# A decode block with a gated MLP on one core: not computing the first layer norm, the product with w1 and its gelu

## The chip, the cores and the metric

The kernel runs on one core of a Trainium2 chip. The metric is the device time of one execution in microseconds (us), lower is better.

## The reference, cut to what matters

```python
x = A_x                                    # (2, 1, 1024): two batch rows, ONE position each
g = sigmoid((x * gate_w).sum(-1, keepdims=True))
a = attention(x, A_k_cache, A_v_cache, A_wq, A_wo)     # 32 heads, 16384 cached keys of 128
b = mixer_mlp(x, B_w1, B_w2, B_w3, B_w4)
return g * a + (1 - g) * b

def mixer_mlp(x, w1, w2, w3, w4):
    B, S, D = x.shape                      # S == 1
    h = gelu(layernorm(x) @ w1)
    c = D // 4
    g0 = pad(h[:, :, 0*c:1*c], ((0,0),(1,0),(0,0)))[:, :S, :]   # shift by +1
    g1 = pad(h[:, :, 1*c:2*c], ((0,0),(0,1),(0,0)))[:, 1:, :]   # shift by -1
    g2 = pad(h[:, :, 2*c:3*c], ((0,0),(2,0),(0,0)))[:, :S, :]   # shift by +2
    g3 = pad(h[:, :, 3*c:   ], ((0,0),(0,2),(0,0)))[:, 2:, :]   # shift by -2
    hs = concatenate([g0, g1, g2, g3], -1) @ w2
    x1 = x + hs
    h2 = gelu(layernorm(x1) @ w3) @ w4
    return x1 + h2
```

All four shifts move along the position axis. With one position every row of `h` is shifted out and zeros come in. So `g0` to `g3` are zero for any `x` and `w1`. The K and V caches are the bulk of the data: 2 x 32 heads x 16384 x 128 in bf16 are 268 MB each. One head of one batch row is 4.19 MB of K and as much of V.

## The kernel before

The kernel walks 64 steps, one per head and batch row. A ring of five SBUF slots of 32 KB per partition (4 MB) takes every large load in a fixed order: K of step g, V of step g-1, and now and then a weight. One queue (SP) issues the loads. It waits for a slot to be released by the engine that read it last.

```python
wloads = {}
...
wloads[("w12", 0)] = [rows4(B_w1, 0, NHI, D), rows4(B_w2, 0, NHI, D, off=W12)]   # two loads, one slot
...
def release(key, ev):          # the slot goes to the next load in the list, which waits for ev
    idx = slot_of[key]
    slot_free[idx] = tuple(ev) if isinstance(ev, (tuple, list)) else (ev,)
    pump()
```

The small MLP is cut into stages that are put between the attention instructions of some steps, at five places of each step:

```python
MPOS = (1, 4, 7, 10, 13)
...
mg = 1
put(mg, [st_gate, ln_a(xT_f[:, :, :], "xT_f", st1_ps, "xn1"), ln_b(st1_ps, "xn1", None)])
mg += 1
key = ("w12", 0)
put(mg, mlp_chain(key, halves, 0, NBD, NBD, h_ps, lambda kc: xn_bf[:, kc, :], "xn1", "h", D, last=False)
    + [gelu1]
    + mlp_chain(key, halves, 0, NBD, NBD, hs_ps, lambda kc: shT_bf[:, kc, :], "const", "hs", D, off=W12), key)
mg += 1
put(mg, [st_x1, ln_a(x1T_f[:, :, :], "x1", st2_ps, "xn2"), ln_b(st2_ps, "xn2", "h")])
```

The kernel already uses constant zeros for the shifted rows (`shT_bf`, set once by a memset). It computes `h` all the same, and nobody reads its result. The slot of w1 and w2 is released by the last product with w2 (`last` is true by default), and K's slot by the last score matmul of the step:

```python
def do_S(g, u):
    ...
    if u == NU - 1:
        ev_S[g] = ev
        release(("k", g), ev)
```

Of the kernel before, what the change touches and what calls it, by code (L numbers as in the profile page):

```python
# [9 lines left out]
BF16 = mybir.dt.bfloat16  # L10
# [75 lines left out]
def build_kernel(nc, A_x, A_k, A_v, A_wq, A_wo, B_w1, B_w2, B_w3, B_w4, gate_w, out, dbg=None):  # L86
    dbg = dbg or {}
    B, Sq, D = A_x.shape
# [4 lines left out]
    P = 128  # L93
# [7 lines left out]
    NBD = D // P  # L101
    NBF = F // P
# [9 lines left out]
    NHI = NBD // R4  # L112
# [5 lines left out]
    with ExitStack() as st:  # L118
        block = st.enter_context(nc.Block())
        sb = lambda name, shape, dt: st.enter_context(nc.sbuf_tensor(name, shape, dt))  # L120
# [14 lines left out]
        xT_f = sb("xT_f", [P, NBD, 2], F32)  # L135
# [17 lines left out]
        mv = sb("mv", [P, 8], F32)  # L153
        zc = sb("zc", [P, NBD, 2], F32)
        xn_bf = sb("xn_bf", [P, NBD, 2], BF16)
        hT_bf = sb("hT_bf", [P, NBD, 2], BF16)
        shT_bf = sb("shT_bf", [P, NBD, 2], BF16)
        x1T_f = sb("x1T_f", [P, NBD, 2], F32)
        GT_bf = sb("GT_bf", [P, NBF, 2], BF16)
# [88 lines left out]
        def rows4(Wt, c0, cn, width, off=0):  # L248
            def fn(e, idx):
                src = Wt[c0 * R4 * P:(c0 + cn) * R4 * P, :].rearrange("(c p r) n -> p c (r n)", p=P, r=R4)  # L250
                dst = ring[:, idx, off:off + cn * R4 * width].rearrange("p (c m) -> p c m", c=cn)
                return e.dma_start(dst, src)
            return fn
# [9 lines left out]
                return e.dma_start(ring[:, idx, 0:hn * D].rearrange("p (h n) -> p h n", h=hn), src)  # L263
            return fn

        W12 = NBD * D
        wloads = {}
        for hi in range(NHI):
            wloads[("wq", hi)] = [rows4(A_wq, hi, 1, HD)]
            wloads[("w3", hi)] = [rows4(B_w3, hi, 1, F)]  # L270
        wloads[("w12", 0)] = [rows4(B_w1, 0, NHI, D), rows4(B_w2, 0, NHI, D, off=W12)]
        w4_parts = _split(NCF, 4)
        for pi, (k0, kn) in enumerate(w4_parts):
            wloads[("w4", pi)] = [rows4(B_w4, k0, kn, D)]
# [16 lines left out]
        B5 = banks[5]  # L291
        a_ps = B5[:, 0:2 * NBD].rearrange("p (n b) -> p n b", b=2)
        c0 = 2 * NBD
        g_ps = B5[:, c0:c0 + 2]; c0 += 4
        st1_ps = B5[:, c0:c0 + 4]; c0 += 4
        st2_ps = B5[:, c0:c0 + 4]; c0 += 4
        h_ps2d = B5[:, c0:c0 + 2 * NBD]; c0 += 2 * NBD
        hs_ps2d = B5[:, c0:c0 + 2 * NBD]; c0 += 2 * NBD
        h2_ps2d = B5[:, c0:c0 + 2 * NBD]; c0 += 2 * NBD
        h3_ps2d = B5[:, c0:c0 + 2 * NBF]; c0 += 2 * NBF  # L300
        assert c0 <= 512
        r3 = lambda ap2: ap2.rearrange("p (n b) -> p n b", b=2)
        h_ps, hs_ps, h2_ps, h3_ps = r3(h_ps2d), r3(hs_ps2d), r3(h2_ps2d), r3(h3_ps2d)
        bc_nb = lambda ap2: ap2.unsqueeze(1).broadcast_to([P, NBD, 2])
        b5_rd = []
        evd = {}
# [16 lines left out]
        def rd5(ev):  # L323
            b5_rd.append(ev)
            return ev
# [18 lines left out]
        def ln_a(z_ap, zkey, st_ps, tag):  # L344
            def run():
                zv = z_ap.rearrange("p n b -> p b n")
                a1 = pl.add("dve", lambda e: e.tensor_reduce(st_in[:, 0:2], zv, axis=AX.X, op=ALU.add),
                            waits=(evd[zkey], evd.get("ln_prev")), sig=True)
                a2 = mm5(st_ps[:, 0:2], ones_f[:, :], st_in[:, 0:2], waits=(a1, ev_const), sig=True)
                a3 = rd5(pl.add("dve", lambda e: e.tensor_scalar(mv[:, 0:2], st_ps[:, 0:2], 1.0 / D, None, op0=ALU.mult),  # L350
                                waits=(a2,) + rd5w(), sig=True))
                a4 = pl.add("dve", lambda e: e.tensor_tensor(zc[:, :, :], z_ap, bc_nb(mv[:, 0:2]), op=ALU.subtract),
                            waits=(a3, evd[zkey], evd.get("zc_free")), sig=True)
                a5 = pl.add("dve", lambda e: e.tensor_tensor(zz[:, 1, :, :], zc[:, :, :], zc[:, :, :], op=ALU.mult),
                            waits=(a4,), sig=True)
                evd[tag + "_a6"] = pl.add("dve", lambda e: e.tensor_reduce(st_in[:, 2:4], zz[:, 1, :, :].rearrange("p n b -> p b n"),
                                                                           axis=AX.X, op=ALU.add), waits=(a5,), sig=True)
                evd[tag + "_a4"] = a4
            return run

        def ln_b(st_ps, tag, xn_free_key):
            def run():
                a7 = mm5(st_ps[:, 2:4], ones_f[:, :], st_in[:, 2:4], waits=(evd[tag + "_a6"],), sig=True)
                a8 = rd5(pl.add("dve", lambda e: e.tensor_scalar(mv[:, 2:4], st_ps[:, 2:4], 1.0 / D, eps, op0=ALU.mult, op1=ALU.add),
                                waits=(a7,) + rd5w(), sig=True))
                a9 = pl.add("pool", lambda e: e.tensor_tensor(mv[:, 4:6], mv[:, 2:4], neg_half[:, :], op=ALU.pow),
                            waits=(a8, ev_const), sig=True)
                evd[tag] = pl.add("dve", lambda e: e.tensor_tensor(xn_bf[:, :, :], zc[:, :, :], bc_nb(mv[:, 4:6]), op=ALU.mult),
                                  waits=(a9, evd[tag + "_a4"], evd.get(xn_free_key)), sig=True)
                evd["ln_prev"] = evd[tag]  # L370
                evd["zc_free"] = evd[tag]
            return run

        def gelu_stage(src_ps2d, n, out_bf2d, src_key, out_key, extra_keys=()):
            def run():
                X = gl_x[:, 0:n]; A0 = gl_a[:, 0:n]; B0 = gl_b[:, 0:n]
                c = math.sqrt(2.0 / math.pi)
                b0 = rd5(pl.add("dve", lambda e: e.tensor_copy(out_bf2d, src_ps2d),
                                waits=(evd[src_key],) + tuple(evd.get(k) for k in extra_keys) + rd5w(), sig=True))
                b1 = pl.add("dve", lambda e: e.tensor_copy(X, out_bf2d), waits=(b0,), sig=True)  # L380
                b2 = pl.add("dve", lambda e: e.tensor_tensor(A0, X, X, op=ALU.mult), waits=(b1,), sig=True)
                b3 = pl.add("dve", lambda e: e.tensor_scalar(A0, A0, 0.044715, 1.0, op0=ALU.mult, op1=ALU.add), waits=(b2,), sig=True)
                b4 = pl.add("dve", lambda e: e.tensor_tensor(B0, A0, X, op=ALU.mult), waits=(b3,), sig=True)
                b5 = pl.add("act", lambda e: e.activation(A0, B0, ACT.Tanh, scale=c), waits=(b4,), sig=True)
                b6 = pl.add("dve", lambda e: e.tensor_scalar(B0, A0, 0.5, 0.5, op0=ALU.mult, op1=ALU.add), waits=(b5,), sig=True)
                evd[out_key] = pl.add("dve", lambda e: e.tensor_tensor(out_bf2d, B0, X, op=ALU.mult), waits=(b6,), sig=True)
            return run
# [38 lines left out]
                               waits=(c2, evd["g"]), sig=True)  # L426

        evd["const"] = ev_const
        gelu1 = gelu_stage(h_ps2d, 2 * NBD, hT_bf[:, :, :].rearrange("p n b -> p (n b)"), "h", "hT")
        gelu2 = gelu_stage(h3_ps2d, 2 * NBF, GT_bf[:, :, :].rearrange("p n b -> p (n b)"), "h3", "GT", ("hT",))  # L430
        MPOS = (1, 4, 7, 10, 13)
        stage_at = {}
        w_at = {}
# [1 line left out]
        def put(g, fns, key=None):  # L435
            if key is not None:
                w_at.setdefault(g, []).append(key)
            assert len(fns) <= len(MPOS)
            for pos, fn in zip(MPOS, fns):
                stage_at.setdefault((g, pos), []).append(fn)  # L440

        def mlp_chain(key, groups, k0, nkw, nout, out_ps, rhs_of, rhs_key, done_key, width, off=0, last=True):
            return [dense_stage(key, kls, k0, nkw, nout, out_ps, rhs_of, rhs_key, done_key, width, off,
                                last and i == len(groups) - 1) for i, kls in enumerate(groups)]

        halves = [list(range(0, NBD // 2)), list(range(NBD // 2, NBD))]
        mg = 1
        put(mg, [st_gate, ln_a(xT_f[:, :, :], "xT_f", st1_ps, "xn1"), ln_b(st1_ps, "xn1", None)])
        mg += 1
        key = ("w12", 0)  # L450
        put(mg, mlp_chain(key, halves, 0, NBD, NBD, h_ps, lambda kc: xn_bf[:, kc, :], "xn1", "h", D, last=False)
            + [gelu1]
            + mlp_chain(key, halves, 0, NBD, NBD, hs_ps, lambda kc: shT_bf[:, kc, :], "const", "hs", D, off=W12), key)
        mg += 1
        put(mg, [st_x1, ln_a(x1T_f[:, :, :], "x1", st2_ps, "xn2"), ln_b(st2_ps, "xn2", "h")])
        MSTEP = 2 if G >= 24 else 1
        for hi in range(NHI):
            mg += MSTEP
            key = ("w3", hi)
# [4 lines left out]
        for pi, (k0, kn) in enumerate(w4_parts):  # L464
            mg += MSTEP
            key = ("w4", pi)
# [40 lines left out]
        last = None  # L507
        for nb in range(NBD):
            last = pl.add("pe", lambda e, nb=nb: e.transpose(tr_ps[:, nb * 4:nb * 4 + 2], xrow4(xg_row, 2, nb), ident[0:2, 0:2]),
                          waits=(ev_x, ev_ident), sig=(nb == NBD - 1))  # L510
# [9 lines left out]
        for hi in range(NHI):  # L520
            key = ("wq", hi)
            ev_arr = arrived(key)
            wv = ring_w(slot_of[key], R4, HD)
            for r in range(R4):
                kc = hi * R4 + r
# [275 lines left out]
```

## Time and profile before

| | before |
|---|---|
| median of 4 runs | 1353.49 us (1352.82 to 1353.92) |
| profiled execution | 1352.0 us, span 1350.2 us |
| read from HBM | 572.53 MB, 424 GB/s over the span |
| PE, DVE, ACT busy | 64%, 56%, 7% |

How to read what follows. A trace tells when each instruction ran and what released it. PE is the matmul engine, DVE, ACT and POOL are the vector, scalar and general engines, SPq is the queue that issues loads. The span runs from the first to the last instruction. A large idle share of an engine says nothing by itself; what matters is which resource has no idle time.

These lines are from the page of the kernel before: the span, the busy share of the 16 DMA engines in 40 equal slices (9 is 90% or more), the total of the reads, the chain of waits that ended last, the transposes of K on DVE (busy us in all, mean ns of one, then DVE's idle time just before them and what ended it), and the two loads w1 and w2 (count, KB each, median us from issue to landing).

```profile
span 1350.2 us, 13016 instructions
...
DMA  9999999999999999999999999999999999999995
...
HBM read 572.53 MB, written 0.00 MB: 424 GB/s over the span
...
DMA 65%; PE 22%; DVE 12%; issue 1%; ACT 0%; SPq 0%; POOL 0%
...
L571 DVE STREAM_TRANSPOSE ring<-ring 128x1024 f32<-128x1024 f32 x512 | 591.7, 1212 | 153.3 <-DMA ring<-in_A_k_cache_dram 153.3
...
ring<-in_B_w_dram SPq DMA_DIRECT2D x2, 2048.0 KB, 43.9
```

DMA is at 9 tenths or more in 39 of 40 slices. The chain is 65% DMA although DMA has no idle slice before the last. The chain follows the data, and where it names PE or DVE, the DMA engines were moving later loads at the same time. The line of the transposes, the first thing done to each K, tells the same from the other side: DVE spent 153.3 us waiting for K to land.

This is the table of stretches of the kernel before. Each row is a stretch in us, its length, the busy time of PE, PE's weight loads, DVE, ACT and POOL with instruction counts, the granted PE clock (1.00 is full speed), the DMA share and GB/s.

```profile
40.00:60.00 20.00, 11.98 (x46) 5.32 (x43) 11.37 (x23) 0.95 (x3) 0.00 (x0) 0.81 0.99 420
60.00:80.00 20.00, 12.02 (x97) 5.40 (x98) 11.00 (x17) 1.38 (x3) 1.19 (x3) 0.76 1.04 443
80.00:100.00 20.00, 15.82 (x162) 7.63 (x163) 11.43 (x21) 1.59 (x4) 0.00 (x0) 0.75 0.99 425
100.00:120.00 20.00, 12.71 (x46) 5.26 (x48) 9.53 (x18) 0.00 (x0) 1.18 (x3) 0.57 1.00 430
400.00:600.00 200.00, 129.61 (x727) 48.17 (x728) 119.56 (x152) 13.76 (x30) 2.62 (x10) 0.83 1.00 431
```

The first four rows hold all the work that the change removes. The last row is the steady state. The DMA share does not tell them apart: it is 0.99 to 1.04 in the first four (a share over 1 cannot be real; presumably it comes from how records are cut at the edge of a stretch) and 1.00 in the last.

This is the timeline of the kernel before around the products with w1 (start, us, engine, line, operation; in brackets the idle time before it and what ended it), and at three later points.

```profile
67.79 0.33 SPq L286 DMA_DIRECT2D ring<-in_A_k_cache_dram  x1
...
73.25 2.37 DVE L571 STREAM_TRANSPOSE ring<-ring 128x1024 f32<-128x1024 f32 x2 [1.33 <-DMA ring<-in_A_k_cache_dram]
...
75.44 1.20 PE L403 MATMUL ps<-xn_bf,ring 128*128 128x2 bf16 x32
...
81.60 1.23 PE L403 MATMUL ps<-xn_bf,ring 128*128 128x2 bf16 x32
...
83.91 0.21 ACT L384 ACTIVATE gl_a<-gl_b 128x16 f32<-128x16 f32 x1 [11.86 <-DVE gl_b L383]
...
93.24 0.33 SPq L289 DMA_DIRECT2D ring<-in_A_v_cache_dram  x1
...
651.85 0.33 SPq L286 DMA_DIRECT2D ring<-in_A_k_cache_dram  x1
...
1341.31 1.91 PE L599 MATMUL ps<-ring,PT_sb 128*32 128x512 bf16 x32 [0.68 <-DMA ring<-in_A_v_cache_dram]
...
1348.58 0.27 SPq L731 DMA_DIRECT2D out_dram<-xg_row  x1
```

### The profile page before, as it was taken

The numbers are of one execution on the slowest core, as the hardware profiler recorded it, in microseconds if no ns is written. First come the engines' busy times: TensorE is split into PE (matmuls) and PEld (weight loads), VectorE is DVE, ScalarE is ACT, GpSimd is POOL, SyncE is SP. The second block draws the span as 40 slices with busy tenths as digits, with TensorE's granted clock in tenths as the row PEclk, the third lists the DMA queues.
The fourth block names the chain that finished last, engine by engine and source line by source line (L and its number), as shares of the span: only waits on it lengthen the run. The fifth ranks groups of instructions, "written<-read, shape, count | busy, mean of one in ns | idle before, by whom it ended". The sixth has DMA issues, their size and how long they took to land.

```text
span 1350.2 us, 13016 instructions
## 1 busy us (share of the span) xinstructions
PE 867.3 (64%) x5734; PEld 349.3 (26%) x5734; DVE 759.2 (56%) x1008; ACT 90.0 (7%) x196; POOL 23.9 (2%) x95
## 2 busy tenths in 40 slices
PE   2676767557666666766674666766666666567546
PEld 2232332223222222222222322222222222222223
DVE  0656455546656656665663656665565566566535
ACT  0000000000000000000000000000000000000000
POOL 1000000000000000000000000000000000000000
PEclk9777666786888878787976978787877887888868
DMA  9999999999999999999999999999999999999995
GB/s 403 427 431 430 432 431 424 435 426 432 432 433 425 432 433 432 429 430 432 432 415 432 429 433 432 430 429 433 432 431 429 432 434 431 429 431 432 415 424 254
DMA packets 24675, 573.38 MB, mean 425 GB/s; under 512 B 2213, under 2 KB 2213, under 8 KB 6314
## 3 DMA queue, kind: packets, MB, share of 16 engines
q1 hardware_dynamic: 24616, 572.54, 99.0%
q8 instruction: 45, 0.74, 0.2%
q14 instruction: 12, 0.10, 0.0%
q10 hardware_dynamic: 2, 0.00, 0.0%
HBM read 572.53 MB, written 0.00 MB: 424 GB/s over the span
## 4 chain that ended last, share of the span: by engine, by line
DMA 65%; PE 22%; DVE 12%; issue 1%; ACT 0%; SPq 0%; POOL 0%
DMA ring<-in_A_k_cache_dram 62%; PE ps L583 16%; DVE ring L571 9%; PE ps L599 3%; DMA ring<-in_A_wq_dram 2%; DMA ring<-in_A_v_cache_dram 2%; PE ps L403 1%; DVE rA L608 1%; PE ps L679 0%; DVE m_sb L620 0%; DVE OT_sb L666 0%; PE ps L615 0%; DVE rmax_bf L610 0%; PE ps L529 0%; PE ps L625 0%
## 5 line engine op out<-in xcount | busy, mean ns | idle before, releaser
L583 PE MATMUL ps<-ring,Z 128*128 128x512 bf16 x2048 | 664.0, 476 | 364.2 <-DVE ring L571 348.3
L571 DVE STREAM_TRANSPOSE ring<-ring 128x1024 f32<-128x1024 f32 x512 | 591.7, 1212 | 153.3 <-DMA ring<-in_A_k_cache_dram 153.3
L583 PEld LDWEIGHTS ps<-ring,Z 128*128 128x128 bf16 x2048 | 206.5, 113 | 719.3 <-DVE ring L571 456.2
L599 PE MATMUL ps<-ring,PT_sb 128*32 128x512 bf16 x2048 | 125.0, 387 | 0.7 <-DMA ring<-in_A_v_cache_dram 0.7
L636 ACT ACTIVATE P_sb<-ps,negm 128x512 bf16<-128x512 f32 x64 | 44.0, 688 | 1180.8 <-DVE negm L630 1180.8
L608 DVE TENSOR_REDUCE rA<-ps 128x1 f32<-128x512 f32 x64 | 44.3, 692 | 122.7 <-PE ps L583 122.7
L666 DVE TENSOR_SCALAR OT_sb<-ps,recip 128x1 bf16<-128x1 f32 x64 | 14.1, 221 | 153.5 <-PE ps L650 153.5
L642 DVE STREAM_TRANSPOSE PT_sb<-P_sb 128x512 bf16<-128x512 bf16 x64 | 45.5, 711 | 54.1 <-ACT P_sb L636 54.1
L599 PEld LDWEIGHTS ps<-ring,PT_sb 128*32 128x32 bf16 x2048 | 49.5, 98 | 45.3 <-issue 3.2
L615 PE MATMUL ps<-ident,rmax_bf 128*1 128x128 bf16 x64 | 14.0, 219 | 66.2 <-DVE rmax_bf L610 66.2
L645 ACT ACTIVATE acc_sb<-ps 128x512 bf16<-128x512 f32 x64 | 38.2, 597 | 53.7 <-PE ps L599 53.7
L564 POOL TENSOR_TENSOR Z<-q_f,mask 128x16 bf16<-128x16 f32 x64 | 16.6, 261 | 1186.8 <-PE ps L583 1166.5
L615 PEld LDWEIGHTS ps<-ident,rmax_bf 128*1 128x1 bf16 x64 | 5.1, 79 | 98.7 <-DVE rmax_bf L610 98.7
L620 DVE TENSOR_REDUCE m_sb<-ps 1x1 bf16<-1x128 bf16 x64 | 18.0, 281 | 19.8 <-PE ps L615 19.8
L650 PEld LDWEIGHTS ps<-dsel,acc_sb 128*128 128x128 bf16 x256 | 20.3, 118 | 33.0 <-issue 29.1
L630 DVE TENSOR_SCALAR negm<-ps,cAB 128x1 f32<-128x1 f32 x64 | 17.8, 278 | 17.2 <-PE ps L625 17.2
L625 PE MATMUL ps<-m_sb,ones_bf 1*128 1x1 bf16 x64 | 11.0, 173 | 24.0 <-DVE m_sb L620 24.0
L657 PEld LDWEIGHTS ps<-rowsum,ones_f 128*128 128x128 f32 x128 | 19.0, 188 | 28.2 <-issue 27.0
L657 PE MATMUL ps<-rowsum,ones_f 128*128 128x1 f32 x128 | 24.5, 260 | 1.2 <-ACT P_sb L636 1.2
L662 DVE RECIPROCAL recip<-ps 128x1 f32<-128x1 f32 x64 | 10.7, 168 | 22.7 <-PE ps L657 22.7
L529 PE MATMUL ps<-xT_bf,ring 128*128 128x2 bf16 x256 | 7.1, 165 | 17.9 <-DMA ring<-in_A_wq_dram 17.9
L650 PE MATMUL ps<-dsel,acc_sb 128*128 128x1 bf16 x256 | 17.4, 172 | 1.1 <-ACT acc_sb L645 1.1
(86 smaller groups left out, 135.5 us busy)
## 6 DMA issues: line engine op xcount, KB each, us to landing
ring<-in_A_k_cache_dram SPq DMA_DIRECT2D x64, 4096.0 KB, 41.2
ring<-in_A_v_cache_dram SPq DMA_DIRECT2D x64, 4096.0 KB, 35.5
ring<-in_A_wq_dram SPq DMA_DIRECT2D x2, 4096.0 KB, 17.4
ring<-in_A_wo_dram SPq DMA_DIRECT2D x2, 4096.0 KB, 44.1
ring<-in_B_w_dram SPq DMA_DIRECT2D x2, 3584.0 KB, 27.0
ring<-in_B_w_dram SPq DMA_DIRECT2D x2, 2048.0 KB, 43.9
ring<-in_B_w_dram SPq DMA_DIRECT2D x1, 4096.0 KB, 34.1
ring<-in_B_w_dram SPq DMA_DIRECT2D x1, 3072.0 KB, 18.9
```

Source lines behind the costliest of these rows:

```text
L571: ev_T[(g, u)] = pl.add("dve", lambda e: e.transpose(ap, ap), waits=(arrived(("k", g)),), sig=True)
L583: ev = pl.add("pe", lambda e, bp=bp: e.matmul(S_ps(pg)[:, 0:NCOL], lhsT=Z[:, pg, bp, ZO - 2 * u:ZO - 2 * u + P], rhs=kv[:, :, bp // 2, :, ...
L599: ev = pl.add("pe", lambda e, jj=jj, hf=hf, cg=cg: e.matmul(acc_ps[32 * cg:32 * cg + 32, 0:512], lhsT=PT_sb[:, pg, 32 * jj:32 * jj + 32], ...
L608: e1 = pl.add("dve", lambda e: e.tensor_reduce(rA[:, pg:pg + 1], S_ps(pg)[:, 0:NCOL], axis=AX.X, op=ALU.max), waits=(ev_S[g],), sig=True)
L615: ev_mt[g] = pl.add("pe", lambda e: e.transpose(mt_ps, rmax_bf[:, pg:pg + 1], ident[:, :]), waits=(ev_rmax[g], ev_m.get(g - 1), ev_ident) ...
L620: ev_m[g] = pl.add("dve", lambda e: e.tensor_reduce(m_sb[0:1, pg:pg + 1], mt_ps, axis=AX.X, op=ALU.max), waits=(ev_mt[g], ev_mb.get(g - 2) ...
L630: ev_negm[g] = pl.add("dve", lambda e: e.tensor_scalar(negm[:, pg:pg + 1], mb_ps, cAB[:, 0:1], cAB[:, 1:2], op0=ALU.mult, op1=ALU.add), wa ...
L636: ev_P[g] = pl.add("act", lambda e: e.activation(P_sb[:, pg, :], S_ps(pg)[:, 0:NCOL], ACT.Exp, bias=negm[:, pg:pg + 1], scale=scale, accum ...
L642: ev_PT[g] = pl.add("dve", lambda e: e.transpose(PT_sb[:, pg, :], P_sb[:, pg, :]), waits=(ev_P[g], ev_PV.get(g - 2)), sig=True)
L645: ev_accc[g] = pl.add("act", lambda e: e.activation(acc_sb[:, :], acc_ps[:, 0:512], ACT.Copy), waits=(ev_PV[g], ev_ext.get(g - 1)), sig=True)
L650: ev = pl.add("pe", lambda e, w=w: e.matmul(oT_ps, lhsT=acc_sb[:, w * P:(w + 1) * P], rhs=dsel[:, w:w + 1], start=(w == 0), stop=(w == 3)) ...
L657: ev_l[g] = pl.add("pe", lambda e: e.matmul(l_ps, lhsT=ones_f[:, :], rhs=rowsum[:, pg:pg + 1], start=True, stop=True), waits=(ev_P[g], ev_ ...
```

## The change

The intent: nothing reads `h`, so do not compute it. The first norm, the product with w1 and the first gelu go, and with them the load of w1. The product with w2 (of zeros) stays. It moves from the last two places of step 2 to the first two.

```diff
--- before.py
+++ after.py
@@ -153,7 +153,6 @@
         mv = sb("mv", [P, 8], F32)
         zc = sb("zc", [P, NBD, 2], F32)
         xn_bf = sb("xn_bf", [P, NBD, 2], BF16)
-        hT_bf = sb("hT_bf", [P, NBD, 2], BF16)
         shT_bf = sb("shT_bf", [P, NBD, 2], BF16)
         x1T_f = sb("x1T_f", [P, NBD, 2], F32)
         GT_bf = sb("GT_bf", [P, NBF, 2], BF16)
@@ -263,12 +262,12 @@
                 return e.dma_start(ring[:, idx, 0:hn * D].rearrange("p (h n) -> p h n", h=hn), src)
             return fn
 
-        W12 = NBD * D
         wloads = {}
         for hi in range(NHI):
             wloads[("wq", hi)] = [rows4(A_wq, hi, 1, HD)]
             wloads[("w3", hi)] = [rows4(B_w3, hi, 1, F)]
-        wloads[("w12", 0)] = [rows4(B_w1, 0, NHI, D), rows4(B_w2, 0, NHI, D, off=W12)]
+
+        wloads[("w2", 0)] = [rows4(B_w2, 0, NHI, D)]
         w4_parts = _split(NCF, 4)
         for pi, (k0, kn) in enumerate(w4_parts):
             wloads[("w4", pi)] = [rows4(B_w4, k0, kn, D)]
@@ -292,15 +291,13 @@
         a_ps = B5[:, 0:2 * NBD].rearrange("p (n b) -> p n b", b=2)
         c0 = 2 * NBD
         g_ps = B5[:, c0:c0 + 2]; c0 += 4
-        st1_ps = B5[:, c0:c0 + 4]; c0 += 4
         st2_ps = B5[:, c0:c0 + 4]; c0 += 4
-        h_ps2d = B5[:, c0:c0 + 2 * NBD]; c0 += 2 * NBD
         hs_ps2d = B5[:, c0:c0 + 2 * NBD]; c0 += 2 * NBD
         h2_ps2d = B5[:, c0:c0 + 2 * NBD]; c0 += 2 * NBD
         h3_ps2d = B5[:, c0:c0 + 2 * NBF]; c0 += 2 * NBF
         assert c0 <= 512
         r3 = lambda ap2: ap2.rearrange("p (n b) -> p n b", b=2)
-        h_ps, hs_ps, h2_ps, h3_ps = r3(h_ps2d), r3(hs_ps2d), r3(h2_ps2d), r3(h3_ps2d)
+        hs_ps, h2_ps, h3_ps = r3(hs_ps2d), r3(h2_ps2d), r3(h3_ps2d)
         bc_nb = lambda ap2: ap2.unsqueeze(1).broadcast_to([P, NBD, 2])
         b5_rd = []
         evd = {}
@@ -426,8 +423,7 @@
                                waits=(c2, evd["g"]), sig=True)
 
         evd["const"] = ev_const
-        gelu1 = gelu_stage(h_ps2d, 2 * NBD, hT_bf[:, :, :].rearrange("p n b -> p (n b)"), "h", "hT")
-        gelu2 = gelu_stage(h3_ps2d, 2 * NBF, GT_bf[:, :, :].rearrange("p n b -> p (n b)"), "h3", "GT", ("hT",))
+        gelu2 = gelu_stage(h3_ps2d, 2 * NBF, GT_bf[:, :, :].rearrange("p n b -> p (n b)"), "h3", "GT")
         MPOS = (1, 4, 7, 10, 13)
         stage_at = {}
         w_at = {}
@@ -445,14 +441,12 @@
 
         halves = [list(range(0, NBD // 2)), list(range(NBD // 2, NBD))]
         mg = 1
-        put(mg, [st_gate, ln_a(xT_f[:, :, :], "xT_f", st1_ps, "xn1"), ln_b(st1_ps, "xn1", None)])
+        put(mg, [st_gate])
         mg += 1
-        key = ("w12", 0)
-        put(mg, mlp_chain(key, halves, 0, NBD, NBD, h_ps, lambda kc: xn_bf[:, kc, :], "xn1", "h", D, last=False)
-            + [gelu1]
-            + mlp_chain(key, halves, 0, NBD, NBD, hs_ps, lambda kc: shT_bf[:, kc, :], "const", "hs", D, off=W12), key)
+        key = ("w2", 0)
+        put(mg, mlp_chain(key, halves, 0, NBD, NBD, hs_ps, lambda kc: shT_bf[:, kc, :], "const", "hs", D), key)
         mg += 1
-        put(mg, [st_x1, ln_a(x1T_f[:, :, :], "x1", st2_ps, "xn2"), ln_b(st2_ps, "xn2", "h")])
+        put(mg, [st_x1, ln_a(x1T_f[:, :, :], "x1", st2_ps, "xn2"), ln_b(st2_ps, "xn2", None)])
         MSTEP = 2 if G >= 24 else 1
         for hi in range(NHI):
             mg += MSTEP
```

## The prediction

> **What bounds the kernel.** The stream of loads. The page counts 572.53 MB read from HBM in a span of 1350.2 us, and its line of slices shows the 16 DMA engines at 9 tenths or more in 39 of 40 slices. In the table of stretches, 400 to 600 us and 800 to 1000 us both give a DMA share of 1.00 and 431 GB/s. The Trainium skill, "DMA: Bandwidth & Descriptors", section "Where 436 GB/s comes from", gives 435.2 GB/s as the fabric's ceiling; this trace, at 431, agrees. PE is busy 64% and DVE 56%. The chain that ended last is 65% DMA, 62% K loads; its PE and DVE pieces are mostly work done while the queue moves later loads, since the DMA share does not fall there. Only the start (first 10 us, share 0.80) and the end (last loads landing about 1337 us, then some 13 us of PE, DVE and store) are not stream.
>
> **What the change removes.**
> - Load: w1, 1024 x 1024 bf16 = 2.10 MB, one of two 2048 KB loads that share a ring slot. At 431 GB/s that is 4.87 us of stream. These loads have 8 KB pieces instead of 32 KB; between 48 and 60 us, where by order the pair should pass, the stretches give about 402 GB/s, which would make it 5.2 us. I take 5.0.
> - PE: 64 matmuls with w1 (two runs of 1.20 and 1.23 us in the timeline) and the first norm's two ones-products (0.28 and 0.42 us).
> - DVE: small norm and gelu operations of 0.12 to 0.18 us, about 2.6 us in all; ACT one tanh, 0.21 us; POOL one power, 0.70 us. The waits around them are 1 to 4 us each.
>
> All this compute lies between 54 and 85 us. The w2 product moves up from the last two of the five places of step 2 to the first two, so its slot comes free earlier. Nothing is added.
>
> **How much is critical.** Of the load, all: the stream is full before, during and after it, and the sequence of slots does not change, since w2's slot is still released before K of its step. Of the compute, nothing: at 67.8 us, when the next slot is freed late, about 13 us of queued loads are still to move by my estimate (two loads outstanding, 9.7 us per 4 MB), and the DMA share stays near 1 from 70 to 110 us. After the change K of step 2 lands some 5 us earlier, and PE and DVE also reach it some microseconds earlier, so the queue should stay fed. From step 3 on everything should run as before, shifted. The tail is the same.
>
> **Predicted time:** 1353.7 - 5.0 = 1348.7 us, range 1347.0 to 1350.4. Chances: faster by over 2% 0.01, within 2% 0.985, slower by over 2% 0.005. The gain, 0.37%, is the share of bytes removed, not of operations.
>
> **What would show it.** Bytes read fall by 2.10 to 570.4 MB, with the mean rate near 424 GB/s; DMA shares near 1.00 between 40 and 120 us; the wait for K of step 2 still ends on a DMA landing, some 5 us earlier; the K issue times of later steps all shifted by about 5 us; an unchanged stretch from the last V landing to the end. Wrong if: the mean rate drops, a stretch between 60 and 110 us falls well below 0.95 (a starved queue), or the shift is later lost.
>
> **What would make it wrong.** A gap in the stream because a slot is freed too late for the shorter queue (gain 2 to 4 us); the 8 KB pieces costing more than I read (gain up to 6); a different granted PE clock in the last 13 us (up to 1 us either way).

## More of the kernel before

At 73.25 us DVE had waited 1.33 us for K of step 2 to land: even in the step that holds the MLP work, the compute engines are ahead of the stream. And the last product with V, released by the last landing, starts 7.3 us before the store of the result: from there on only compute is left.

## The result, and the profile after

A ratio below is the mean time of one kernel's fast runs over the mean of the other's fast runs in the same rounds, so it is not quite the ratio of the medians quoted beside it.

| | before | after |
|---|---|---|
| median of 4 runs | 1353.49 us (1352.82 to 1353.92) | 1347.57 us (1346.95 to 1349.49) |
| profiled execution, span | 1350.2 us | 1345.2 us |
| read from HBM | 572.53 MB | 570.43 MB |
| mean rate over the span | 424 GB/s | 424 GB/s |

The ratio is 0.9959, with a 95% interval of 0.9942 to 0.9976: faster by about 0.4%. The spans of the two profiled executions differ by 5.0 us. The medians differ by 5.9 us, the means by 5.5; the control run below did not repeat the excess.

The same lines of the page of the changed kernel:

```profile
span 1345.2 us, 12862 instructions
...
DMA  9999999999999999999999999999999999999995
...
HBM read 570.43 MB, written 0.00 MB: 424 GB/s over the span
...
DMA 65%; PE 24%; DVE 10%; issue 1%; ACT 0%; POOL 0%; SPq 0%
...
L565 DVE STREAM_TRANSPOSE ring<-ring 128x1024 f32<-128x1024 f32 x512 | 591.5, 1212 | 156.9 <-DMA ring<-in_A_k_cache_dram 156.9
...
ring<-in_B_w_dram SPq DMA_DIRECT2D x1, 2048.0 KB, 41.5
```

The table of stretches of the changed kernel, same columns:

```profile
40.00:60.00 20.00, 14.31 (x52) 6.14 (x51) 14.48 (x21) 0.95 (x3) 0.26 (x1) 0.74 1.00 429
60.00:80.00 20.00, 13.54 (x130) 6.50 (x128) 10.96 (x15) 1.37 (x3) 0.26 (x1) 0.70 1.01 434
80.00:100.00 20.00, 12.45 (x77) 5.47 (x75) 9.44 (x21) 1.38 (x3) 0.79 (x2) 0.84 0.99 425
100.00:120.00 20.00, 14.04 (x79) 5.22 (x80) 14.63 (x19) 1.38 (x3) 0.40 (x2) 0.86 1.01 431
400.00:600.00 200.00, 130.46 (x733) 48.91 (x732) 121.36 (x155) 13.75 (x30) 2.62 (x10) 0.82 1.00 430
```

The DMA share stays at 0.99 or more in every row, so the stream has no gap. Over the 80 us together PE and DVE are not less busy (PE 54.3 us against 52.5 before, DVE 49.5 against 43.3), although work was removed: later attention work has moved forward into these windows.

The timeline of the changed kernel, with the lines that answer to those of before:

```profile
61.99 0.33 SPq L285 DMA_DIRECT2D ring<-in_A_k_cache_dram  x1
...
68.20 2.37 DVE L565 STREAM_TRANSPOSE ring<-ring 128x1024 f32<-128x1024 f32 x2 [2.08 <-DMA ring<-in_A_k_cache_dram]
...
71.19 1.23 PE L400 MATMUL ps<-shT_bf,ring 128*128 128x2 bf16 x32
...
84.52 0.33 SPq L288 DMA_DIRECT2D ring<-in_A_v_cache_dram  x1
...
646.92 0.33 SPq L285 DMA_DIRECT2D ring<-in_A_k_cache_dram  x1
...
1336.26 1.91 PE L593 MATMUL ps<-ring,PT_sb 128*32 128x512 bf16 x32 [0.63 <-DMA ring<-in_A_v_cache_dram]
...
1343.53 0.27 SPq L725 DMA_DIRECT2D out_dram<-xg_row  x1
```

This is the most telling comparison. The K load of step 2 was waited for until 73.25 us before and until 68.20 us after: 5.05 us earlier. The same K issue deep in the kernel moved from 651.85 to 646.92, 4.93 us. The last product with V moved from 1341.31 to 1336.26, 5.05 us, and the store from 1348.58 to 1343.53, again 5.05 us. The whole gain is there at 68 us, before one product with w2 has run, and nothing is added to it or lost from it in the next 1270 us. In between, the compute engines gained more than that for a while: the slot of K of step 2 was released (the V issue at that time takes it) at 93.24 us before and at 84.52 us after, 8.7 us earlier. The 3.7 us beyond the 5.05 bought nothing. They turned into longer waits for the stream. DVE's next wait for a K ended at 140.05 us before and at 135.03 us after, 5.02 us earlier, and had lasted 2.21 us before and 8.13 us after. At K of step 2 it was 2.08 us instead of 1.33, and over the whole kernel 156.9 us instead of 153.3 in the line of the transposes, 3.6 us more.

### The profile page after: what moved, and what is told of

It reads as the page before. It is cut to its first block, busy times and chain, and to the rows that moved or that the text cites. A ratio compares the mean times of both kernels' runs of the same rounds, so it can differ in the third digit from the quotient of the medians.

```text
span 1345.2 us, 12862 instructions
## 1 busy us (share of the span) xinstructions
PE 864.8 (64%) x5666; PEld 347.8 (26%) x5666; DVE 757.0 (56%) x994; ACT 89.7 (7%) x195; POOL 23.3 (2%) x94
## 3 DMA queue, kind: packets, MB, share of 16 engines
HBM read 570.43 MB, written 0.00 MB: 424 GB/s over the span
## 4 chain that ended last, share of the span: by engine, by line
DMA 65%; PE 24%; DVE 10%; issue 1%; ACT 0%; POOL 0%; SPq 0%
DMA ring<-in_A_k_cache_dram 62%; PE ps L577 18%; DVE ring L565 7%; PE ps L593 3%; DMA ring<-in_A_wq_dram 2%; DMA ring<-in_A_v_cache_dram 2%; PE ps L400 1%; DVE rA L602 1%; PE ps L673 1%; DVE m_sb L614 0%; DVE OT_sb L660 0%; PE ps L609 0%; DVE rmax_bf L604 0%; PE ps L523 0%; PE ps L619 0%
## 5 line engine op out<-in xcount | busy, mean ns | idle before, releaser
L565 DVE STREAM_TRANSPOSE ring<-ring 128x1024 f32<-128x1024 f32 x512 | 591.5, 1212 | 156.9 <-DMA ring<-in_A_k_cache_dram 156.9
L624 DVE TENSOR_SCALAR negm<-ps,cAB 128x1 f32<-128x1 f32 x64 | 17.7, 277 | 17.3 <-PE ps L619 17.3
## 6 DMA issues: line engine op xcount, KB each, us to landing
ring<-in_A_wo_dram SPq DMA_DIRECT2D x2, 4096.0 KB, 43.3
```

Source lines behind the costliest of these rows:

```text
L565: ev_T[(g, u)] = pl.add("dve", lambda e: e.transpose(ap, ap), waits=(arrived(("k", g)),), sig=True)
L624: ev_negm[g] = pl.add("dve", lambda e: e.tensor_scalar(negm[:, pg:pg + 1], mb_ps, cAB[:, 0:1], cAB[:, 1:2], op0=ALU.mult, op1=ALU.add), wa ...
```

## The experiments

The theory under test (the **stream theory**): the time is the bytes over the rate of the stream, plus a fixed start and end, so the 2.10 MB of w1 are the whole gain and the removed compute is worth nothing. The rivals: **A**, the compute of steps 1 and 2 held up PE and so the release of slots; **B**, the bytes give most and the compute the rest; **C**, the load that went had covered for slots freed late, and its absence starves the queue.

### The changed kernel again, as a yardstick

No edit. Run beside the next three, on the same chip.

> The changed kernel again, beside the three variants, as their yardstick. Stream theory (the time is the bytes moved at the rate of the stream): 5.0 us below the kernel before, ratio 0.9963. If the larger gain of the first runs (5.9 us between the medians) is more than scatter, it should be near 5.9 again.

Measured: 1348.97 us median of 5 (before: 1353.90 of 9), ratio 0.9965, interval 0.9952 to 0.9979. The means differ by 4.94 us (1348.65 against 1353.59). The 5.9 us of the first runs was not repeated; 5.0 us is the size, as far as runs with this scatter tell.

### The load kept, the compute gone

```diff
-        wloads[("w2", 0)] = [rows4(B_w2, 0, NHI, D)]
+        W12 = NBD * D
+        wloads[("w2", 0)] = [rows4(B_w1, 0, NHI, D), rows4(B_w2, 0, NHI, D, off=W12)]
 ...
-        put(mg, mlp_chain(key, ..., lambda kc: shT_bf[:, kc, :], "const", "hs", D), key)
+        put(mg, mlp_chain(key, ..., lambda kc: shT_bf[:, kc, :], "const", "hs", D, off=W12), key)
```

> Loads w1 beside w2 as the kernel before does, but computes nothing from it. Stream theory: as slow as the kernel before, within 0.5 us of it, ratio 1.000. Rival A (the first norm, product and gelu of steps 1 and 2 hold up PE and so the slots): about as fast as the changed kernel, 5 us below before. Rival B (bytes give most, compute a rest): 0.5 to 1.5 us below before.

Measured: 1353.55 us median of 5, ratio 1.0000, interval 0.9986 to 1.0014. The result is correct. Taking away all the compute gains 0.3 us by the means (1353.25 against 1353.59), which the interval of plus or minus 1.9 us does not tell from zero. The timeline of this kernel has the same K issue as that quoted above at 651.82 us, where the kernel before has 651.85:

```profile
651.82 0.33 SPq L286 DMA_DIRECT2D ring<-in_A_k_cache_dram  x1
```

Where the removed compute went is seen on DVE. These are the line of the transposes on the page of this kernel, and the wait for K of step 2 in its timeline:

```profile
L566 DVE STREAM_TRANSPOSE ring<-ring 128x1024 f32<-128x1024 f32 x512 | 591.5, 1212 | 165.9 <-DMA ring<-in_A_k_cache_dram 165.9
...
73.19 2.37 DVE L566 STREAM_TRANSPOSE ring<-ring 128x1024 f32<-128x1024 f32 x2 [8.35 <-DMA ring<-in_A_k_cache_dram]
```

K of step 2 was waited for until 73.19 us, as before (73.25), but DVE had waited 8.35 us for it and not 1.33. Over the whole kernel it waited 165.9 us for K instead of 153.3: the time freed on DVE became waiting.

Rival A falls. The times alone do not exclude rival B. In the profiled run the equal position of the issue, to 0.03 us, and an equal end (spans 1350.3 and 1350.2 us) leave it no room.

### The compute kept, the load gone

Everything that the kernel before computes, in the same places. Only w1 is not loaded; the first product reads w2 where it read w1. Its values are wrong and are dropped, as those of `h` always were.

```diff
-        W12 = NBD * D
 ...
-        wloads[("w12", 0)] = [rows4(B_w1, 0, NHI, D), rows4(B_w2, 0, NHI, D, off=W12)]
+        wloads[("w12", 0)] = [rows4(B_w2, 0, NHI, D)]
 ...
-            + mlp_chain(key, ..., lambda kc: shT_bf[:, kc, :], "const", "hs", D, off=W12), key)
+            + mlp_chain(key, ..., lambda kc: shT_bf[:, kc, :], "const", "hs", D), key)
```

> Computes all that the kernel before computes, in the same places, but loads only w2 and lets the first product read w2 in the place of w1; its values are dropped, so the result stays right. Stream theory: as fast as the changed kernel, 5.0 us below before. Rival A: as slow as before. Rival C (with 5 us less of queued loads the late slots of steps 1 to 3 starve the queue): 1 to 4 us slower than the changed kernel, with a stretch of the DMA share clearly under 0.95 between 60 and 120 us.

Measured: 1349.05 us median of 5, ratio 0.9964, interval 0.9950 to 0.9977; correct. Its mean, 1348.68 us, is that of the changed kernel (1348.65) to 0.03 us, closer than the scatter warrants. The traces agree: the last product with V starts at 1336.25 us here (line below) and at 1336.26 in the changed kernel. So the load alone gives the whole gain. This kernel has w2's product at the old, late places, so moving it forward in the change did nothing measurable either. Rival C falls for this size of change: the DMA share is 0.99 to 1.01 in every 20 us stretch from 40 to 120 us.

One reading shows where scatter of a microsecond or two comes from. In the timeline of this profiled execution the last product with V took nearly twice as long as in the runs shown above, and the table of stretches gives the clock there:

```profile
1336.25 3.60 PE L598 MATMUL ps<-ring,PT_sb 128*32 128x512 bf16 x32 [2.49 <-DMA ring<-in_A_v_cache_dram]
```

```profile
1336.00:1340.00 4.00, 3.60 (x32) 1.24 (x32) 0.00 (x0) 0.10 (x1) 0.00 (x0) 0.50 0.02 4
```

The granted clock was 0.50 (the third figure from the right in the line of the table), and the 32 matmuls took 3.60 us instead of 1.91. The Trainium skill, "TensorE: Matmul & The Clock Gate", section "Part 1: The HAM clock gate", describes two states of the clock, half rate after idle time and full rate after sustained work. This trace agrees in the size of the step: 3.60 over 1.91 is 1.9. Here PE had been idle for 2.49 us before. That a longer wait for V leads to the slow product is a pattern of the profiled runs, and not tested by an edit: of the thirteen, the last product took 1.91 us in eight (PE had not waited for V in five of them, and 0.63, 0.68 and 1.58 us in the others) and 2.93 to 3.61 us in the five where it had waited 1.31 to 3.13 us. Within the stream such a slow spell is hidden (in the kernel before the clock was 0.57 from 100 to 120 us, at a DMA share of 1.00). In the tail it counts in full: from the start of this product to the end of the span it is 11.05 us here and 8.94 in the changed kernel, 2.1 us more, which is the whole difference of the two spans (1347.3 and 1345.2).

### Without w2 as well

The same argument goes one step further: the product of zeros with w2 is zero (for finite w2), so `x1` is `x`.

```diff
-        wloads[("w2", 0)] = [rows4(B_w2, 0, NHI, D)]
 ...
-            evd["x1"] = rd5(pl.add("dve", lambda e: e.tensor_tensor(x1T_f[:, :, :], xT_f[:, :, :], hs_ps, op=ALU.add),
-                                   waits=(evd["hs"], evd["xT_f"]) + rd5w(), sig=True))
+            evd["x1"] = pl.add("dve", lambda e: e.tensor_copy(x1T_f[:, :, :], xT_f[:, :, :]), waits=(evd["xT_f"],), sig=True)
 ...
-        key = ("w2", 0)
-        put(mg, mlp_chain(key, halves, 0, NBD, NBD, hs_ps, lambda kc: shT_bf[:, kc, :], "const", "hs", D), key)
```

> Drops the product with w2 as well, with its load and its slot: the shifted rows are all zero, so the sum is x. Stream theory: another 2.10 MB, another 4.9 to 5.0 us, 9.9 us below before, ratio 0.9927. Rival A: the product with w2 is 64 matmuls like that with w1, but no chain of norm and gelu, so 1 to 3 us more than the changed kernel at most.

Measured: 1343.24 us median of 5, ratio 0.9924, interval 0.9910 to 0.9937, and correct. That is 10.4 us below before by the means (1343.15 against 1353.59), and 5.5 us below the changed kernel; 5.0 was expected. A second set of five on another chip, as the yardstick of a later run:

> The kernel without w1 and w2 again, as the yardstick of the next run: 9.9 to 10.7 us below the kernel before, as in its first runs.

Measured: 1343.66 us median of 5 (before: 1353.02 of 9), ratio 0.9930, interval 0.9917 to 0.9942; 9.5 us by the means (1343.59 against 1353.08), just outside the 9.9 to 10.7 expected. The two sets bracket the 9.9 us that two loads of 2.10 MB should be worth.

### What a byte costs, by the size of its piece

The prediction took 5.0 us for w1, between 4.87 us (at the steady 431 GB/s) and 5.2 us (at 402 GB/s, read off a stretch of 12 us). The open point was whether pieces of 8 KB per partition run slower than the 32 KB of the K loads. Eight dead loads of the same 4.19 MB each, in three shapes, make it large enough to see. Each load takes a slot in the second half of the kernel, is touched by one small matmul that writes unused PSUM columns, and is released.

```diff
+        ND = 8
+        def dead_rows(i):                 # r=128, c=1: 32 KB pieces; r=32, c=4: 8 KB; r=8, c=16: 2 KB
+            src = A_k[0, i].rearrange("(c p r) d -> p c (r d)", p=P, r=128)
+            return lambda e, idx: e.dma_start(ring[:, idx, :].rearrange("p (c m) -> p c m", c=1), src)
+        for i in range(ND):
+            wloads[("dead", i)] = [dead_rows(i)]
 ...
+        dead_ps = B5[:, 508:510]
+        def dead_stage(i):
+            def run():
+                ev = pe_b5(lambda e: e.matmul(dead_ps, lhsT=ring[:, slot_of[("dead", i)], 0:P], rhs=ones_bf[:, 0:2],
+                                              start=False, stop=True, skip_group_check=True),
+                           waits=(arrived(("dead", i)), ev_const), sig=True)
+                b5_wrote(ev)
+                release(("dead", i), ev)
+            return run
+        for i in range(ND):
+            put(44 + 2 * i, [dead_stage(i)], ("dead", i))
```

> The changed kernel with eight more loads of 4.19 MB in the second half, of parts of K, each touched by one small matmul and dropped; one piece of 32 KB per partition. 33.55 MB at 431 GB/s: 77.9 us above the changed kernel (about 72.9 above before).

> The same eight loads of the same bytes, but in pieces of 8 KB, as w1 was loaded. If the 402 GB/s read between 48 and 60 us is the rate of 8 KB pieces: 83.5 us above the changed kernel, 5.6 more than with 32 KB pieces. If the size of a piece does not matter at this size: 77.9 us, the same as with 32 KB pieces within 1 us.

> The same bytes in pieces of 2 KB, as wo is loaded. The two slices with a wo load move 415 instead of 432 GB/s, an estimate of 1.3 us more per 4.19 MB: 88 us above the changed kernel, some 10 more than with 32 KB pieces. If the dip of these slices has another cause: 77.9.

All three gave correct results, on one chip, with the kernel before at 1353.19 us (7 runs, mean 1353.03). The last two columns are worked out: the mean above before, plus the 4.94 us that the changed kernel saved in the control (on another chip), is the cost of the 33.55 MB; the bytes over it give the rate.

| pieces | median of 4 | ratio to before | cost of 33.55 MB | rate |
|---|---|---|---|---|
| 32 KB | 1426.05 us | 1.0539 (1.0523 to 1.0554) | 77.9 us | 431 GB/s |
| 8 KB | 1428.02 us | 1.0553 (1.0535 to 1.0571) | 79.9 us | 420 GB/s |
| 2 KB | 1434.54 us | 1.0603 (1.0587 to 1.0619) | 86.6 us | 387 GB/s |

The 32 KB case hit its expectation to the tenth (72.9 us above before by the medians); with intervals of about 2 us to either side the tenth is luck. That is the stream theory at sixteen times the dose. The 8 KB pieces cost about 2 us more, not 5.6: the expectation from the 402 GB/s is a miss, that reading was a short stretch with edges and no rate of 8 KB pieces. The intervals of the first two rows overlap, so the times alone do not show that 8 KB pieces are slower at all. They also contain the tail: the last product with V took 1.91 us in the profiled run with 32 KB pieces, but 2.93 with 8 KB and 3.60 with 2 KB. The issue times in the traces are free of the tail. The same K issue, the fourth after the last dead load, falls at 1303.16 us with 32 KB, at 1304.55 with 8 KB and at 1311.02 with 2 KB pieces. So the 8 KB pieces cost 1.4 us more and the 2 KB pieces 7.9, in one profiled run each; before the first dead load the three differ by about 1 us in either direction. At 420 GB/s w1 costs 79.9 / 16 = 5.0 us, at 431 it costs 4.87. The 2 KB pieces cost 8.7 us more than 32 KB by the times, clear of the scatter, and near the 10 expected. The layout changed with the size (one, four or sixteen separate pieces per partition), so the two were not told apart.

The table of stretches for the 320 us with most of the dead loads, in the kernel with 32 KB and then in that with 2 KB pieces:

```profile
880.00:1200.00 320.00, 172.90 (x969) 64.36 (x967) 159.07 (x202) 17.88 (x39) 3.42 (x13) 0.78 1.00 431
```

```profile
880.00:1200.00 320.00, 169.66 (x948) 64.93 (x946) 152.53 (x197) 17.87 (x39) 3.40 (x13) 0.74 1.01 422
```

The DMA share is full in both; the same engines, always busy, move less with small pieces (the average is diluted by the K and V loads between). A full share is therefore not a full rate.

### How much compute the step can hide

If removed compute is worth nothing, added compute should cost nothing until the queue runs dry. Two doses: three or twelve more products of zeros with w2 in step 2 (the results stay right, since they add zero), w2's slot released after the last.

```diff
-        put(mg, mlp_chain(key, ..., "const", "hs", D), key)
+        put(mg, mlp_chain(key, ..., "const", "hs", D, last=False), key)
+        alln = list(range(NBD))
+        NX = 4                                    # 1 in the small dose
+        for i in range(3 * NX):
+            stage_at.setdefault((mg, MPOS[2 + i // NX]), []).append(
+                dense_stage(key, alln, 0, NBD, NBD, hs_ps, lambda kc: shT_bf[:, kc, :], "const", "hs", D, last=(i == 3 * NX - 1)))
```

> The changed kernel with three more products of zeros with w2 in step 2 (192 matmuls, about 2.5 us of PE each, 7.4 us in all; w2's slot is released after the last). The estimate: the loads queued at step 2 last to about 98 us and the step ended at 84.5 us, so 7.4 us more fit: no change against the changed kernel, 5 us below before. If PE time in this step is critical: up to 7 us slower than the changed kernel.

> The same with twelve more products (768 matmuls, about 29.5 us of PE). The estimate: 13.5 us of cover are used up and the stream stands still for the rest, so 12 to 16 us slower than the changed kernel, with a stretch of the DMA share far under 0.9 near 100 to 115 us. If the cover is larger than I read, less; if PE time counts in full, 29.

Small dose: 1348.37 us median of 4 (before: 1353.02 of 9), ratio 0.9966, interval 0.9952 to 0.9980. This is the changed kernel's ratio (0.9965): 192 more matmuls cost nothing.

Large dose: 1366.81 us median of 4, ratio 1.0099, interval 1.0085 to 1.0112. That is 17.9 us above the small dose by the means (1366.44 against 1348.50), more than the 12 to 16 expected, and less than the full 29. Its timeline shows the last load issued before a long pause and the first after it, and its table of stretches the gap that follows from it:

```profile
64.48 0.33 SPq L288 DMA_DIRECT2D ring<-in_A_v_cache_dram  x1
...
112.28 0.33 SPq L285 DMA_DIRECT2D ring<-in_A_k_cache_dram  x1
```

```profile
90.00:94.00 4.00, 4.00 (x49) 2.27 (x48) 0.00 (x0) 0.00 (x0) 0.00 (x0) 0.59 1.01 434
94.00:96.00 2.00, 2.00 (x65) 2.00 (x64) 0.00 (x0) 0.00 (x0) 0.00 (x0) 1.00 0.68 287
96.00:112.00 16.00, 15.40 (x416) 14.22 (x415) 0.00 (x0) 0.00 (x0) 0.00 (x0) 0.52 0.01 3
112.00:114.00 2.00, 1.98 (x12) 0.51 (x9) 0.00 (x0) 0.00 (x0) 0.00 (x0) 0.50 0.82 221
```

The queue ran dry at about 95.3 us (287 of 431 GB/s in the stretch from 94 to 96 is 1.3 us of stream) and moved again at about 113.0 us (221 of 431 in the next 2 us). The gap is 17.7 us, and the kernel lost 17.9 (agreement to 0.2 us is closer than the scatter). What the stream lost was not earned back. The expectation was off mainly in one term: it took the cover to last to 98 us, and it ended at 95.3.

This also gives the margin of the change. The 95.3 us hold for the loads issued up to 64.48 us, with w1 already gone. In the yardstick run of the changed kernel the next slot, that of w2, was taken by a K at 78.64 us, and K's slot of step 2 was released at 85.31 us, 10 us before the cover would have ended. So the missing load could not starve the queue. The closest call was the kernel that kept the compute and dropped the load: it had issued the same loads, and its next K issue came at 91.36 us, by this estimate 4 us before the queue would have run dry, and its DMA share was still 0.99. The small dose, at 90.96 us, was as close. So with w2's product left late, rival C failed by a few microseconds only.

### Work after the end of the stream

The same kind of saving in the tail, as the counterpart: in the kernel without w1 and w2, the last copy of the output row is cut in two halves on ACT and DVE. Each half has a PSUM bank of its own.

```diff
-        o_ps = bank_bf(0)[0:2, 0:D]
+        o_half = (bank_bf(1)[0:2, 0:R4 * P], bank_bf(0)[0:2, 0:R4 * P])
 ...
+        for c, eng in ((0, "act"), (1, "dve")):
+            ...  # four transposes into o_half[c], then
+            if eng == "act":
+                fn = lambda e, dst=dst, src=src: e.activation(dst, src, ACT.Copy)
+            else:
+                fn = lambda e, dst=dst, src=src: e.tensor_copy(dst, src)
```

> Without w1 and w2, and with the last copy of the output row (2.41 us of one VectorE instruction, after the last load has landed) cut into two halves on ScalarE and VectorE. Theory: work after the end of the stream counts in full, so about 1.2 us below the run before it, 11 to 12 us below the kernel before, and the stretch from the last products with V to the store shorter by that much. Rival (small compute is worth nothing in this kernel, wherever it stands): no change of that stretch.

The timeline of the run without the split, from the transposes on:

```profile
1336.83 0.61 PE L715 MATMUL ps<-ident,outT_bf 128*2 128x128 bf16 x8 [0.58 <-DVE outT_bf L709]
1337.47 2.41 DVE L718 COPY xg_row<-ps 2x1024 bf16<-2x1024 bf16 x1 [0.70 <-PE ps L715]
1339.91 0.27 SPq L721 DMA_DIRECT2D out_dram<-xg_row  x1
```

The timeline of the run with it:

```profile
1336.08 0.61 PE L718 MATMUL ps<-ident,outT_bf 128*2 128x128 bf16 x8 [0.59 <-DVE outT_bf L709]
1336.50 1.29 ACT L723 ACTIVATE xg_row<-ps 2x512 bf16<-2x512 bf16 x1 [2.06 <-PE ps L718]
1336.72 1.28 DVE L725 COPY xg_row<-ps 2x512 bf16<-2x512 bf16 x1 [0.70 <-PE ps L718]
1338.10 0.27 SPq L727 DMA_DIRECT2D out_dram<-xg_row  x1
```

From the first transpose to the store it is 3.08 us without and 2.02 us with the split: 1.06 us less, nearly all of it from the copy (2.41 to 1.28 us). Measured: 1342.59 us median of 5, ratio to before 0.9923, interval 0.9910 to 0.9937, correct. The medians of the two kernels differ by 1.07 us and the means by 1.1, near the 1.2 expected; the 11 to 12 us below before were missed, since the yardstick itself stood at 9.5. Their intervals overlap, so the times alone do not show it; the trace does. This is the fastest kernel, about 10.6 us (0.8%) below before.

## Why the prediction was right

It forecast 1348.7 us, with 1347.0 to 1350.4 as the range. The first runs gave 1347.57, the control 1348.97. Point by point:

- **The stream bounds the kernel.** Shown. Load alone gone: 0.9964. Compute alone gone: 1.0000. Both gone: 0.9965. Eight more loads cost their bytes at 431 GB/s.
- **The load is worth 5.0 us.** Shown. 4.94 us in the control, 5.05 us between the profiled timelines. The term was taken between 4.87 and 5.2; the piece-size runs put it at 4.9 to 5.0. The reason for its upper end, that 8 KB pieces run at 402 GB/s, was wrong: they run at about 420. In the stretch read for it the DMA share was 0.95, and the next 20 us showed 443 GB/s.
- **The compute is worth nothing.** Shown to about 2 us by the times (interval of the kernel that kept only the load), and to about 0.1 us in the profiled runs, whose K issue at 651.8 us and whose end did not move.
- **The queue stays fed.** Shown. The shares stayed at 0.99 or more. The large dose of products measured some 10 us of cover at the release of K's slot of step 2; the estimate behind that dose was 13.5, so the cover was overestimated, harmlessly.
- **Everything later is only shifted, and the tail is the same.** Shown. The shift was 5.05 us at 68 us, 4.93 at 652 us and 5.05 at the end. The tail was mis-sized without harm: the prediction has the last loads landing at about 1337 us and 13 us after it, but the product that waits for the last V starts at 1341.31, and 8.9 us follow, before and after alike. The tail is not the same in every run, though. In the yardstick's profiled run the last product started at 1337.28 without waiting for V, since PE was still busy with the step before, and its span was 1.0 us longer than the first one of the same kernel.
- **What could go wrong.** The granted clock in the tail was named as worth up to 1 us. It is worth 1.7 us in the last product alone (3.60 against 1.91 us) and 2.1 us to the end of the kernel. It did not matter between the two profiled runs, whose last products took 1.91 us each; that is luck, as five of thirteen profiled runs had the slow product.

What stays open: whether the compute gave some tenths of a microsecond, which runs that scatter by 1 to 3 us cannot tell; and why the first set of runs showed 5.9 us. The half-clock tail is a source of scatter of the right size, but it is not shown to be the cause in those runs, since they were not all profiled.

## What to carry to other kernels

When the load engines have no idle slice, price a change by its bytes at the measured rate of the stream and by what it does to the tail. Here removed compute was worth nothing within the stream, and added compute cost nothing until the queue ran dry, after which each microsecond counted. Look at an early landing and a late one in both timelines: if the shift is the same in both, the gain was made by the first and not touched again up to the second. And if a value is provably zero or unused, follow the zeros to the next weight: here the load of w2 was worth as much again as that of w1.

## What the Trainium skill lacked or had wrong

- "DMA: Bandwidth & Descriptors", "Where 436 GB/s comes from": the ceiling of 435.2 GB/s is borne out (431 GB/s for 200 us on end), but the same section says that for loads from HBM the HBM side, about 358 GB/s, binds, and notes beside it a measured 425, near the fabric's rate. For one core alone it does not bind: all these loads come from HBM, at 431 GB/s in the steady state. "HBM Reference", "Specifications (TRN2)", has it right, with about 425 for a core that streams alone; the mean over the span here is 424.
- "DMA: Bandwidth & Descriptors", "Specifications": 512 B is given as the least transfer for line rate. On the SP queue, pieces of 2 KB per partition ran at about 387 GB/s against 431 for 32 KB pieces of the same bytes (8.7 us on 33.55 MB), with the DMA share full in both. The page's measured table goes by the size of a whole load and from another queue; a table of trn2 rates by piece size on this queue, for loads of one size, is missing.
- "TensorE: Matmul & The Clock Gate", "Part 1": agrees on the size of the step, and lacks a hint for kernels bound by loads: in these runs slow spells cost nothing while the stream was full (clock 0.57 from 100 to 120 us at a DMA share of 1.00), and 1.7 us in the last product after it (3.60 against 1.91 us).
